# Batch 1's fourth turn, the first two pairs' sums and batch 3's turns moved by a few slots in a fused attention and MoE kernel

## The chip, the cores and the metric

The kernel runs on one core of a Trainium2 chip. The metric is the device time of one execution in microseconds (us). All times of single instructions below come from one profiled execution. The engines are called PE (matrix products; PEld is its weight load), DVE (VectorE), ACT (ScalarE), POOL (GpSimd) and SP (SyncE, which issues DMAs here).

## What is computed

Attention over 8 batches, 8 heads, 576 positions of 64 numbers, with a sliding window of 128 positions and a linear bias per head, then two matrix products with an ELU between them.

```python
def _attn_ref(q, k, v) -> np.ndarray:
    B, H, S, D = q.shape
    window = 128
    scale = 1.0 / np.sqrt(D)
    scores = scale * np.matmul(q, k.transpose(0, 1, 3, 2))
...
    mask = (rel >= 0) & (rel < window)
    scores = np.where(mask, scores + bias[None], -1000000000.0)
    scores = scores - np.max(scores, axis=-1, keepdims=True)
    attn = np.exp(scores)
    attn = attn / (np.sum(attn, axis=-1, keepdims=True) + 1e-09)
    return np.matmul(attn, v).astype(np.float32)

def _moe_ref(x, w_in, w_out) -> np.ndarray:
    h = x @ w_in
    alpha = 1.0
    g = np.where(h > 0.0, h, alpha * (np.exp(np.minimum(h, 0.0)) - 1.0))
    return (g @ w_out).astype(np.float32)
```

The attention output, 4608 tokens of 512 numbers, is x; w_in is 512 by 2048 and w_out is 2048 by 512.

## The kernel before

Attention and the two products are interleaved by hand. The order is a list of slots, numbered from 0. A slot holds, in this order: exponentials of scores (`before`), one hidden step (`HID`, function `hidden`), the ELU of the slot before (`done`, which calls `elu`), the slot's tasks (`at`, in the order in which they were entered; `at_once` puts a task in front of all those entered so far), output products (`OUT`) and what comes last (`after`). Every engine takes its instructions in the order in which the slots issue them, and a semaphore holds an instruction until its inputs are there and its target is free.

The parts of a slot that matter here:

- **Hidden step** (L305): 512 columns of x times w_in, into one of two PSUM banks, hp0 and hp1, in turn. ACT turns it into e, by two activations (L312, L313) in the slots of the set `SOFT`, or by one (L315) with POOL's clamp (L316) in the others. DVE's `elu` (L323) makes g from e and the bank, and so frees the bank for the step two slots later.
- **Output products** of a pair of token tiles (L393, `product`). Pair n is 256 tokens; seven products take the place of eight, from sums of blocks of g (`sums`: S1 to S4 on DVE, L354) and of w_out (`quarters`: T1 to T4). The order of a pair's products is 1, 2, 6, 5, 7, 3, 4, seven block products to a slot. Product 6 needs S2, product 5 S1, product 7 S3, product 3 S4. ACT copies some results to U tiles (L396), and `combine` adds them into the output tile (C11, C12, C22; L354 with the target ob), which SP sends out (L412).
- **Attention.** The scores of a unit of 128 keys go to banks spa, sp2, sp3 (L176 for batch 1, L225 later); ACT takes exponentials (L205 and L210, L233 and L236); DVE multiplies them by a table (`first_weigh`, L216; `weigh`, L241); PE multiplies them with the values (L253, L271) with the sum of the weights as a last column; DVE makes the norm (rden, L259 or L276) and scales (xn, L260 or L277).
- **turn** (L281 to L290) transposes the finished tile xn into xT, the hidden steps' input: through PE (L289) and a copy by ACT (L290), or by a DMA transpose from SP (L285). Batch 1's tiles 0 to 3 go through PE, tile 3 by the bank sp3.
- **turn_qk** (L145): DVE transposes q and k of batches 2 and up in 32 by 32 blocks; four instructions for a batch: k in two halves, q in two halves.

Pair n has its slots from 15 + 8n on: pair 2 has slots 31 to 39. Pair 1 has the nine slots (19, 20, 21, 22, 23, 25, 27, 29, 30). A pair's S1 stands in the slot before its first, S2, S3 and S4 in its slots number 1, 3 and 4 (counted from 0), C22 in number 8. Batch 1's units are worked on in slots 18 to 32; batch 2's units start in slot 31 and batch 3's in slot 48. `START` gives the slot in which the scores of a batch's first unit are issued, `TURN` the slots in which q and k of batches 2 and 3 are turned; later batches take slots from `START`. POOL issues the loads of q, k and v.

Of the kernel before, what the change touches and what calls it, by code (L numbers as in the profile page):

```python
# [18 lines left out]
def kernel(  # L19
# [9 lines left out]
    nc = tc.nc  # L29
# [47 lines left out]
    sp = [spa[:, 0, :], spa[:, 1, :]] + [ps_s.tile([128, 512], F32, name=f"sp{i}", tag=f"sp{i}") for i in (2, 3)]  # L77
    hp = [ps_h.tile([128, 512], F32, name=f"hp{i}", tag=f"hp{i}") for i in range(2)]
    av = ps_v.tile([128, 512], F32, name="av", tag="av")
# [69 lines left out]
    with tc.manual_schedule():  # L149
# [343 lines left out]
        def at(s, f, *a):  # L493
            tasks.setdefault(s, []).append((f, a))

        def at_once(s, f, *a):
            tasks.setdefault(s, []).insert(0, (f, a))

        def after(s, f, *a):
            late.setdefault(s, []).append((f, a))  # L500
# [81 lines left out]
        for u, a0, a1, d in ((0, 18, 19, 2), (1, 20, 21, 2), (2, 22, 24, 0), (3, 26, 28, 0)):  # L582
            for half, a in enumerate((a0, a1)):
                at(a, first_scores, 1, u, half, d * half)
                at(a, first_expo, 1, u, half, d * half, 0, 256)
                at(a + 1, first_weigh, 1, u, half)
                at(a + 2, values, 1, u, half, av if half else sp[2])
            at(a1 + 3, turn, 1, u, nc.scalar.copy, (av, av, av, sp[3])[u])
        at(25, turn_first, 1, 1, 1, 0, av, nc.scalar.copy)
        at(30, values, 1, 4, 0, sp[2])  # L590
        at(31, values, 1, 4, 1)
# [2 lines left out]

        START = [None, None, 31, 48, 66, 83, 100, 117]

        TURN = [None, None, (22, 24, 25, 28), (40, 42, 44, 46)]
        REST = 32, 33, 36, 37
        for b in range(2, B):
            for u in range(4):  # L600
# [13 lines left out]
            for n in range(4):  # L614
                piece = (b, int(n < 2), n % 2)
                if b == 2:
                    m = 4 if n < 2 else 6
                    at(TURN[b][n], turn_qk, *piece, 0, m)
                    at(REST[n], turn_qk, *piece, m, R)
                else:  # L620
                    at(TURN[b][n] if b == 3 else a + 4 * n, turn_qk, *piece)
            for n in range(8):
# [8 lines left out]
        for n in SEVEN:  # L631
            s = 15 + 8 * n
            ps = (19, 20, 21, 22, 23, 25, 27, 29, 30) if n == 1 else range(s, s + 9)
            if n < 2 * NTB - 1:
                for d, i in ((-1, 1), (1, 2), (3, 3), (4, 4)):
                    at_once(ps[d] if d > 0 else ps[0] - 1, sums, n, i)
                after(ps[2], combine, n, "C11")
                after(ps[6], combine, n, "C12")
                at_once(ps[8], combine, n, "C22")
                for d in range(8):  # L640
                    OUT[ps[d]] = [(product, (n, i, j, j + 1)) for i, j in turns[7 * d:7 * d + 7]]
            else:
                at_once(s - 3, sums, n, 3)
                for i in (2, 1):
                    at_once(s - 2, sums, n, i, 0, 6)
                    at_once(s - 1, sums, n, i, 6, 8)
                at(s - 1, product, n, 1)
                OUT[s] = [(product, (n, 2)), (combine, (n, "C11")), (sums, (n, 4)), (product, (n, 6)), (product, (n, 5))]
                OUT[s + 1] = [(product, (n, 7)), (product, (n, 3)), (combine, (n, "C22")), (combine, (n, "C12")),
                              (product, (n, 4)), (last_out, (n,))]  # L650
# [48 lines left out]
```

## Time and profile before

| | us |
|---|---|
| median of 4 runs | 311.41 |
| lowest, highest | 310.97, 313.57 |
| the profiled execution | 311.59 |
| its span (first to last instruction) | 309.8 |

TensorE's granted clock is 1.00 in all of it. Two of the costliest groups of instructions, and the ones that the change moves:

```profile
L305 PE MATMUL hp<-xT,wi 128*128 128x256 f16 (+3 forms) x1488 | 144.3, 245 | 1.3 <-DVE g L323 1.0
L323 DVE SCALAR_TENSOR_TENSOR g<-e,hp 128x512 f16<-128x512 f32 x138 | 93.8, 679 | 23.3 <-ACT e L313 12.8
L354 DVE TENSOR_TENSOR S<-g 128x1024 f16<-128x1024 f16 (+2 forms) x35 | 23.6, 673 | 0.8 <-PE op L393 0.2
```

A line of a group gives the source line, the engine, the operation, target and inputs with their sizes, the count, then the busy time in us and the mean of one in ns, and last the idle time of the engine just before, with what ended most of it. A line of a timeline gives start, duration, engine, source line and tiles, and in square brackets how long the engine had been idle and which instruction released it. A line of the chain of waits gives the start and length of a piece of the chain that ended last. In a table of stretches each engine has its busy time and its number of instructions, followed by the clock, the share of the DMA engines and the rate in GB/s.

Durations of neighbours on one engine overlap a little, so the distance from one start to the next is what an instruction takes from its engine: the g of 0.68 us takes 0.60. In time, slot 18 begins at about 48 us, slot 31 at 69, slot 35 at 79, slot 48 at 105.

### The profile page before, as it was taken

What the parts mean: (1) busy time and instruction counts of PE and PEld (TensorE: products, weight loads), DVE (VectorE), ACT (ScalarE), POOL (GpSimd) and SP (SyncE); (2) the same over time, 40 slices, a digit from 0 to 9 for tenths busy, and PEclk for the clock granted to TensorE, in tenths of its full rate; (3) what the DMA queues carried; (4) which work ended last, traced back from release to release, by engine and by line L of the source; (5) the groups of instructions that cost most, each with busy time, mean ns of one, the idle gap of its engine ahead of it and who ended that gap; (6) DMA issues with size and microseconds to landing.
All of it is one profiled execution on the core that took longest, in us unless ns stands there. A gap on an engine that the chain in (4) does not pass through costs nothing.

```text
span 309.8 us, 9820 instructions
## 1 busy us (share of the span) xinstructions
PE 299.7 (97%) x4071; PEld 256.2 (83%) x4071; DVE 257.9 (83%) x498; ACT 241.8 (78%) x446; POOL 108.7 (35%) x163
## 2 busy tenths in 40 slices
PE   7899999998999999999999999999999999999995
PEld 5688875797888888988888888888899888898884
DVE  4646879988989999897989998989998788886782
ACT  4576678677888698879797889788888797968871
POOL 8847858374251415140706060706000001010000
PEclk9999999999999999999999999999999999999999
DMA  9999999999094949495979997999630302230103
GB/s 97 177 200 199 202 187 185 104 115 114 19 153 72 134 73 148 55 142 69 112 89 122 126 96 84 129 130 111 66 98 5 95 17 87 19 97 0 70 27 111
DMA packets 96509, 32.04 MB, mean 103 GB/s; under 512 B 83920, under 2 KB 91984, under 8 KB 96464
## 3 DMA queue, kind: packets, MB, share of 16 engines
q0 software_dynamic: 75920, 18.36, 64.1%
q1 hardware_dynamic: 20400, 12.98, 17.5%
q8 instruction: 32, 0.52, 0.7%
q14 instruction: 13, 0.11, 0.1%
q10 hardware_dynamic: 144, 0.07, 0.1%
HBM read 36.70 MB, written 9.44 MB: 149 GB/s over the span
## 4 chain that ended last, share of the span: by engine, by line
PE 76%; DVE 7%; ACT 7%; DMA 3%; issue 3%; POOL 3%; POOLq 0%; ACTq 0%; DVEq 0%
PE hp L305 34%; PE op L393 13%; PE av L393 13%; PE spa L225 4%; DVE g L323 3%; DMA s<-in_q_dram 3%; PE spa L271 3%; PE sp L393 2%; ACT EX L236 2%; PE op L329 1%; POOL e L316 1%; PE sp L305 1%; ACT e L315 1%; PE sp L253 1%; ACT e L312 1%
## 5 line engine op out<-in xcount | busy, mean ns | idle before, releaser
L305 PE MATMUL hp<-xT,wi 128*128 128x256 f16 (+3 forms) x1488 | 144.3, 245 | 1.3 <-DVE g L323 1.0
L305 PEld LDWEIGHTS <-wi 128*128 128x128 f16 x1600 | 119.7, 98 | 18.3 <-issue 6.7
L323 DVE SCALAR_TENSOR_TENSOR g<-e,hp 128x512 f16<-128x512 f32 x138 | 93.8, 679 | 23.3 <-ACT e L313 12.8
L316 POOL TENSOR_SCALAR e<-e 128x512 f32<-128x512 f32 x44 | 28.1, 639 | 157.8 <-ACT e L315 152.9
L312 ACT ACTIVATE e<-hp 128x512 f32<-128x512 f32 x98 | 58.6, 598 | 28.7 <-PE hp L305 24.2
L313 ACT ACTIVATE e<-e 128x512 f32<-128x512 f32 x100 | 63.1, 631 | 3.2
L393 PEld LDWEIGHTS <-S 128*128 128x128 f16 x544 | 51.4, 98 | 6.1 <-issue 0.5
L393 PEld LDWEIGHTS <-g 128*128 128x128 f16 x408 | 38.2, 98 | 4.8 <-issue 0.6
L241 DVE TENSOR_TENSOR EX<-EX,TAB 128x1024 f16<-128x1024 f16 x48 | 33.0, 687 | 6.4 <-ACT EX L236 3.7
L114 POOL DMA_DIRECT2D VP<-in_v_dram x40 | 34.5, 874 | 2.1 <-DMA s<-in_k_dram 1.0
L315 ACT ACTIVATE e<-hp 128x512 f32<-128x512 f32 x40 | 24.1, 601 | 10.4 <-PE hp L305 10.4
L393 PE MATMUL op<-T,S 128*128 128x256 f16 x200 | 30.0, 273 | 0.0
L233 ACT ACTIVATE EX<-spa 128x1024 f16<-128x1024 f32 x24 | 24.6, 1025 | 4.4 <-PE spa L225 4.1
L393 PE MATMUL av<-T,S 128*128 128x256 f16 x176 | 26.4, 272 | 0.1
L236 ACT ACTIVATE EX<-sp 128x512 f16<-128x512 f32 x48 | 26.0, 596 | 0.0
L354 DVE TENSOR_TENSOR S<-g 128x1024 f16<-128x1024 f16 (+2 forms) x35 | 23.6, 673 | 0.8 <-PE op L393 0.2
L393 PE MATMUL op<-wo,g 128*128 128x256 f16 x128 | 19.2, 273 | 0.1
L393 PE MATMUL av<-wo,g 128*128 128x256 f16 x120 | 18.0, 273 | 0.0
L277 DVE TENSOR_TENSOR xn<-spa,rden 128x512 f16<-128x512 f32 x24 | 16.6, 692 | 0.8
L108 POOL DMA_DIRECT2D st<-in_k_dram x24 | 16.2, 686 | 2.8 <-DMA s<-in_q_dram 2.1
L108 POOL DMA_DIRECT2D st<-in_q_dram x24 | 15.9, 666 | 0.8 <-DMA VP<-in_v_dram 0.6
L271 PE MATMUL spa<-VP,EX 128*128 128x65 f16 x336 | 15.2, 193 | 0.1
(139 smaller groups left out, 379.7 us busy)
## 6 DMA issues: line engine op xcount, KB each, us to landing
out_dram<-ob SPq DMA_DIRECT2D x35, 256.0 KB, 2.5
VP<-in_v_dram POOLq DMA_DIRECT2D x32, 128.0 KB, 5.6
st<-in_k_dram POOLq DMA_DIRECT2D x24, 144.0 KB, 5.1
st<-in_q_dram POOLq DMA_DIRECT2D x24, 144.0 KB, 5.9
wi<-in_moe_w_in_dram POOLq DMA_DIRECT2D x4, 512.0 KB, 12.0
wo<-in_moe_w_out_dram POOLq DMA_DIRECT2D x4, 512.0 KB, 11.2
VP<-in_v_dram POOLq DMA_DIRECT2D x8, 64.0 KB, 5.8
s<-in_k_dram POOLq DMA_DIRECT2D x1, 512.0 KB, 13.2
```

Of the source, the lines that this page charges most:

```text
L108: nc.gpsimd.dma_start(st[b][32 * g:32 * g + 32, w, :, :, :, :].rearrange("p h n j d -> p (h n) (j d)"), (q, k)[w][b, 2 * g:2 * g + 2, :, : ...
L114: nc.gpsimd.dma_start(VP[b % 2][0:p, n, :, 0:D], v[b, :, 128 * n:128 * n + p, :].rearrange("h p d -> p h d"))
L233: nc.scalar.activation(unit(b, u)[:, 0:2, :, :], spa.rearrange("p g (h c) -> p g h c", h=2), AF.Exp, scale=0.125)
L236: nc.scalar.activation(unit(b, u)[:, g, :, :], sp[g].rearrange("p (h c) -> p h c", h=2), AF.Exp, scale=0.125)
L241: V.tensor_tensor(out=e, in0=e, in1=TAB[:, int(u == 3), 2 * gp:2 * gp + 2, :, :], op=ALU.mult)
L305: nc.tensor.matmul(p[:, l * w + u0:l * w + u1], w_in_sb[:, c, fc * 128:(fc + 1) * 128], xT[:, c, x0:x0 + u1 - u0], start=(c == 0), stop=(c ...
L312: nc.scalar.activation(e[:, 0:n], p[:, 0:n], AF.Relu, scale=-1.0)
L313: nc.scalar.activation(e[:, 0:n], e[:, 0:n], AF.Exp, scale=-1.0)
L315: nc.scalar.activation(e[:, 0:n], p[:, 0:n], AF.Exp)
L316: nc.gpsimd.tensor_scalar(out=e[:, 0:n], in0=e[:, 0:n], scalar1=1.0, scalar2=0.0, op0=ALU.min, op1=ALU.max)
L323: V.scalar_tensor_tensor(out=gs[t][:, f0:f0 + nf, c0:c0 + w], in0=sh(es.pop((t, c0, f0))), scalar=1.0, in1=sh(hps.pop((t, c0, f0))), op0=A ...
L393: nc.tensor.matmul(o, a[:, j, :], b[:, j, :], start=j == 0 and i in (1, 2, 5), stop=j == 7, skip_group_check=True)
```

## The change

Three edits, each in the order alone:

```diff
-            at(a1 + 3, turn, 1, u, nc.scalar.copy, (av, av, av, sp[3])[u])
+            at(a1 + 3 + u // 3, turn, 1, u, nc.scalar.copy, (av, av, av, sp[3])[u])
...
-        TURN = [None, None, (22, 24, 25, 28), (40, 42, 44, 46)]
+        TURN = [None, None, (22, 24, 25, 28), (35, 39, 43, 47)]
...
-                    at_once(ps[d] if d > 0 else ps[0] - 1, sums, n, i)
+                    (at_once if n > 2 else at)(ps[d] if d > 0 else ps[0] - 1, sums, n, i)
...
-                at_once(ps[8], combine, n, "C22")
+                (at_once if n > 2 else at)(ps[8], combine, n, "C22")
```

- Batch 1's tile 3 (u is 3, so u // 3 is 1) is turned in slot 32 instead of 31: four transposes on PE and one copy on ACT. The hidden steps that read this tile begin in slot 34.
- Batch 3's k halves are turned on DVE in slots 35 and 39 instead of 40 and 42, its q halves in 43 and 47 instead of 44 and 46.
- The sums S1 to S4 and C22 of pairs 1 and 2, the second and third pair, come behind the other tasks of their slot instead of ahead of them: behind the weights and norms of the attention units. From pair 3 on they stay ahead.

One consequence for what is computed: the turn in slot 32 writes the first half of bank sp3 after batch 2's first unit has put its scores there (end of slot 31) and before the exponential of slot 33 reads them. For one head of that unit the exponentials are then taken of the transposed bits, not of the scores. The number and size of all instructions stay as they were.

## The prediction

> **What bounds the kernel now.** I read the page first, then the stretches by time, then the chain of waits and the timelines of DVE, ACT and PE where the change acts. Page, busy time and the chain by engine:
>
> ```profile
> PE 299.7 (97%) x4071; PEld 256.2 (83%) x4071; DVE 257.9 (83%) x498; ACT 241.8 (78%) x446; POOL 108.7 (35%) x163
> ...
> PE 76%; DVE 7%; ACT 7%; DMA 3%; issue 3%; POOL 3%; POOLq 0%; ACTq 0%; DVEq 0%
> ```
>
> PE carries the end, so the change can only be worth the gaps of PE in the slots it touches. The stretches (PE, PEld, DVE, ACT, POOL busy) show where these are:
>
> ```profile
> 48.00:58.00 10.00, 9.28 (x114) 6.45 (x111) 9.38 (x21) 7.44 (x13) 6.04 (x8) 1.00 1.93 178
> 58.00:69.00 11.00, 11.00 (x226) 10.14 (x224) 9.08 (x19) 8.63 (x15) 7.82 (x12) 1.00 0.80 95
> 69.00:83.00 14.00, 12.84 (x197) 10.90 (x194) 12.57 (x26) 11.08 (x21) 3.58 (x5) 1.00 0.68 78
> 83.00:94.00 11.00, 11.00 (x144) 9.67 (x142) 9.76 (x20) 9.40 (x18) 6.34 (x9) 1.00 1.22 133
> 94.00:107.00 13.00, 12.51 (x171) 10.71 (x172) 12.61 (x26) 9.54 (x19) 4.70 (x7) 1.00 0.74 91
> ```
>
> The slots touched by the pairs (18 to 24 and 30 to 39) and by batch 3's turns (35 to 47) lie in rows one, three and five. PE is idle there for 0.72, 1.16 and 0.49 us, 2.4 in all: a ceiling of 0.8% of the span. In the same rows DVE is 94%, 90% and 97% busy, so DVE, not PE, is the engine with no room. The largest gap, from the whole timeline:
>
> ```profile
> 68.50 0.69 DVE L323 SCALAR_TENSOR_TENSOR g<-e,hp 128x512 f16<-128x512 f32 x1 [0.51 <-POOL e L316]
> ...
> 69.22 0.69 DVE L354 TENSOR_TENSOR S<-g 128x1024 f16<-128x1024 f16 x1
> ...
> 69.33 1.06 POOL L316 TENSOR_SCALAR e<-e 128x512 f32<-128x512 f32 x1 [0.24 <-ACT e L315]
> 69.83 0.83 DVE L354 TENSOR_TENSOR ob<-U,U 128x256 f32<-128x256 f32 x1
> ...
> 70.59 0.17 DVE L259 RECIPROCAL rden<-av 128x4 f32<-128x4 f32 x1
> ...
> 70.79 0.42 DVE L260 TENSOR_TENSOR xn<-av,rden 128x256 f16<-128x256 f32 x1
> ...
> 71.27 0.34 PE L289 MATMUL sp<-ident,xn 128*128 128x128 f16 x3 [0.92 <-DVE xn L260]
> ```
>
> Pair 2's first sum S1 and pair 1's C22 stand ahead of batch 1's norms, and PE's turn of the fourth tile waits 0.92 for them. In slots 42 to 46, by the chain of waits:
>
> ```profile
> 95.14 0.40 DVE xn L277
> 95.54 0.21 issue
> 95.75 0.77 DVE KT L145
> 96.52 0.58 DVE g L323
> 97.10 0.04 issue
> 97.15 1.03 PE hp L305 x8
> ...
> 102.99 0.69 DVE xn L277
> 103.68 0.21 DVE QT L145
> 103.89 0.39 issue
> 104.28 0.66 DVE g L323
> 104.95 0.04 issue
> 104.99 1.03 PE hp L305 x8
> ```
>
> Here a turn of batch 3 on DVE (0.77) delays the elu g that frees the bank of PE's next hidden step: twice a third of a microsecond.
>
> **The change part by part.** No instruction is added or removed. The instruction order of the changed program shows 493 instructions on DVE and 442 on ACT as before; POOL's and SP's orders are the same, so no DMA is passed. I replay the order with steps from one start to the next in the timeline: g, S and weigh 0.60, rden 0.20, xn of 256 columns 0.34, ob 0.34, full turn 0.69; on PE a hidden step 0.89, a product 0.11; on ACT L290 0.46.
>
> *A, pair 1 (slots 18 to 24).* S2 (50.19) goes behind the norms and the second weigh of unit 0. That norm waits for PE until 50.96 anyway, so the weigh still starts at 51.52. S2 then ends near 52.8; its product starts at 53.04. The next norms and weigh slip 0.11 (PE +0.1). S3 at 54.08 no longer stands ahead of unit 1's second weigh, which would end 0.25 earlier, so the gap before PE's values at 55.98 (0.47) halves. But S3 now ends near 56.6, and its product, at 56.66 before, waits for that. Taken: 0. Bounds: -0.35 (if S3 fits in) to +0.15 (the slip stays). S4 and C22 are used one or more slots later; their cover is that distance.
>
> *B, slots 30 to 35.* DVE after the g of 68.50: rden, xn, rden, xn at 69.22, 69.42, 69.76, 69.96; C22 at 70.30, S1 at 70.64, the g of slot 30 at 71.25, ending 71.93 (72.3 before). PE no longer turns in slot 31: values at 70.13 instead of 71.45, products 70.37, scores 71.23, hidden step of slot 32 not at its natural 71.79 but at 72.0, when that g is done; 73.11 before. So 1.1 earlier. What is late next: the turn's four matmuls (0.22) now come after that step, and ACT's copy L290 has left a place where ACT idled (0.98 before the 73.22 exponential) for one where ACT runs without a gap until 79.9: behind it are U1, the exponentials L236 of sp2 and sp3, then two pairs L312/L313. L236 starts at 75.0 to 75.1 instead of 75.63, the weigh at 76.15 (76.75), C11 at 77.2 (77.79), and PE's product that waits for C11 at 77.6 (78.22). Of 1.1 us, 0.5 goes to L290's step, and 0.6 remains.
>
> One size is open, C22's. The row has 0.83, every other such ob 0.41 or 0.42, while POOL's e beside it took 1.06 instead of 0.61. The Trainium skill ("SBUF — State Buffer", section "SBUF: two separate sides") says that a VectorE operation with two SBUF inputs and a GpSimd one that reads SBUF hold a shared port pair in turn, for the whole instruction. By that e, now beside norms that read PSUM, ends near 70.0, before C22 starts at 70.30, and C22 costs 0.41: -0.6. By the row alone, 0.83 again: -0.2. I take -0.6; bounds -0.9 (the whole wait of L289) to +0.45 (rival 2). The same rule speaks against the change further on: with PE and DVE shifted unequally, the e of slots 36, 44 and 45 would start during a weigh; in before they ran beside others and took 0.61. The rule would hold each until the weigh ends, 0.3 to 0.45; the rows of such meetings (e at 64.14 and 67.67, during a weigh) show 0.84 and 0.80, so 0.2 each. I take the rows' 0.2.
>
> *C, batch 3's turns.* Slot 35 takes a turn of 0.69 ahead of S4 and g. With B's lead the g of slot 34 ends near 80.2, K's turn 80.8, S4 81.4, g 82.1; PE wants that bank at 82.2. The 0.39 and 0.28 that DVE idles at 82.39 and 83.65 pay for it. S4's product comes 0.55 into slot 36, at 81.9: covered. Slot 39's turn lies behind slot 38's g, which PE needs only 0.9 later. In slot 42 nothing stands between xn and g any more: PE's step of slot 44 starts at its natural 96.73 less 0.6, not 97.15: another 0.4. In slot 46 likewise 0.33. Together a lead of 1.3 at slot 48. It can't all stay: DVE has as much to do up to slot 48 as before, and Q's last turn is now in slot 47, right ahead of that slot's g. DVE's own lead is what its idle times give. The g of slot 45 (101.42) came after two waits for e and can be 1.0 early, less 0.2 for the port: 0.8. From there to the g of slot 48 (108.16) DVE runs without a break, and PE needed that g 0.12 after its end: a lead of 0.9. So C adds 0.3. Bounds: -0.7 to +0.2 (all idle time of DVE used, or Q's turn holding batch 3's first scores). K's and Q's loads cover: issued by 70.34, and landing takes 8.1 at most.
>
> *Later.* From slot 49 on both programs are alike, and PE is 92.75 of 93 and 99.8 of 100 us busy: a lead is kept. The fourth tile's turn writes half of bank sp3 between batch 2's scores and their exponential; an exponential's time does not depend on its numbers in any row, so nothing is charged.
>
> Sum: 0 - 0.6 - 0.3 = -0.9 us. Against the profiled execution, 311.59 (span 309.8 and 1.8 around it): 310.7. That run lies 0.18 over the median of 311.41, so 310.5.
>
> **The rivals.**
> 1. *DVE is the bound, and the lead is eaten.* For it: 12.61 of 13 us busy in the fifth row. B's lead falls to 0.2 (C22 at 0.83), C gives it back: 311.2, between 310.9 and 311.5. Against it: 2.4 us of waits that the timeline shows on DVE between 70 and 102, which an earlier PE shortens.
> 2. *L290 in front of the exponentials: slower.* Place: ACT in slot 32. Price: 0.46, since U1, L236, the weigh, C11 and PE's product follow it one by one. It decides if the hidden step of slot 32 starts less than 0.46 earlier, thus if g of slot 30 ends after 72.6 (a longer C22, or a later e). With nothing of the lead left it costs up to 0.45, and with A's +0.15: 312.0. Against it: 0.7 us between 71.93 and that point.
> 3. *The change does not do what it says*: pair 1 gains nothing because its norms wait for PE, not DVE. That is in the sum already; without B's gain too it is 311.4, counted with rival 1.
>
> **How the numbers follow.** Forecast 0.62 (own range 309.9 to 311.0), rivals 1 and 3 together 0.24, rival 2 0.14. Predicted 310.5. The range, 309.6 to 312.0, reaches down nearly to the three lower bounds together (-1.95, 309.5) and takes in rival 1 whole and rival 2 up to its price; what it leaves out is part C at its upper bound on top of rival 2. About 1% (3.1 us) is what a measurement of this kernel can tell from no change. Faster by that needs more than the 2.4 us of gaps: 0.02. Slower by it needs a wait that comes back in each of many slots, where the diff touches three short stretches: 0.04. Within 1%: 0.94.
>
> **What would show it.** B right: no wait of L289 for xn, C22 at 0.41, the hidden step of slot 32 about 1.1 earlier, PE's product after C11 0.6 earlier. C right: no wait of L305 for g at slots 44 and 48, and about 0.9 of lead at 109. A right: S3 the last wait in slot 23. Wrong if PE gains at 56 or if L236 of slot 33 is not earlier. The forecast as a whole is wrong if PE shows new gaps after 110, which I hold for alike.

## The result, and the profile after

| | before | after |
|---|---|---|
| median, us | 311.87 (64 runs) | 310.98 (43 runs) |
| lowest, highest | 310.92, 313.57 | 309.88, 313.55 |
| profiled execution, its span | 311.59, 309.8 | 313.29, 311.5 |

The ratio of after to before is 0.9971, 95% interval 0.996 to 0.9981: 0.9 us less. With more runs than the prediction had, the median of before is 311.87, not 311.41, so the forecast 310.5 stands 0.5 below what was measured although the difference of 0.9 is the one forecast.

The profiled execution of the changed kernel is longer than that of before, and this has to be understood first. Its first hidden steps already start 2.7 us late, in code that the change does not touch. So all comparisons below are made slot by slot: the start of the hidden step's first matmul, counted from the hidden step of slot 17 in the same execution (44.49 us before, 47.16 after), minus the same for before. From slot 1 to slot 17 this difference is within 0.02 us in all kernels of this study; what happens ahead of slot 1 drops out. Kernels with the same edits in a stretch agree there to 0.02 as well (slots 32 to 36 of the change and of two of the kernels below).

| slot | 24 | 32 | 33 | 35 | 36 | 43 | 44 | 46 | 48 | 50 | 76 | 149 |
|---|---|---|---|---|---|---|---|---|---|---|---|---|
| after, us | +0.03 | -1.22 | -1.01 | -0.75 | -0.62 | -0.61 | -1.02 | -0.79 | -1.11 | -0.93 | -0.95 | -0.97 |

The stretches of before that had PE's gaps, in the changed kernel (the same slots, shifted by the start and by what was gained; columns as before):

```profile
50.70:60.70 10.00, 9.50 (x114) 6.36 (x110) 8.99 (x21) 7.44 (x13) 4.35 (x6) 1.00 1.73 159
71.70:85.00 13.30, 13.06 (x197) 10.80 (x193) 12.42 (x27) 11.09 (x21) 3.13 (x5) 1.00 0.76 83
96.10:108.70 12.60, 12.55 (x174) 10.59 (x172) 11.74 (x25) 9.49 (x19) 5.01 (x7) 1.00 0.78 94
```

PE idles 0.50, 0.24 and 0.05 us there (0.72, 1.16 and 0.49 before). This idle time is not the gain: in the first row 0.22 of it is gone although slot 24 starts no earlier, because the wait is now one of the weight loads (shown under part A), which PE's column does not count. Slot 31 in the timeline of after, PE, DVE and ACT:

```profile
71.20 0.69 DVE L323 SCALAR_TENSOR_TENSOR g<-e,hp 128x512 f16<-128x512 f32 x1 [0.50 <-POOL e L316]
...
71.81 0.18 DVE L259 RECIPROCAL rden<-av 128x4 f32<-128x4 f32 x1
...
72.83 0.41 PE L253 MATMUL av<-VP,EX 128*128 128x65 f16 x8
72.90 0.41 DVE L354 TENSOR_TENSOR ob<-U,U 128x256 f32<-128x256 f32 x1
...
73.83 0.67 DVE L323 SCALAR_TENSOR_TENSOR g<-e,hp 128x512 f16<-128x512 f32 x1
...
74.56 1.05 PE L305 MATMUL hp<-xT,wi 128*128 128x128 f16 x16
```

The norm follows g at once, no wait stands beside PE's values, C22 (ob) takes 0.41 instead of 0.83, and the hidden step of slot 32 starts 2.62 us after that of slot 31 (71.94) instead of 3.87. It starts 0.06 after the end of the g of slot 30: that is its last wait. In slot 44:

```profile
97.20 0.69 DVE L277 TENSOR_TENSOR xn<-spa,rden 128x512 f16<-128x512 f32 x1
97.80 0.68 DVE L323 SCALAR_TENSOR_TENSOR g<-e,hp 128x512 f16<-128x512 f32 x1
...
98.80 1.05 PE L305 MATMUL hp<-xT,wi 128*128 128x256 f16 x8
```

No turn stands between xn and g, and g is done 0.3 before PE asks.

### The profile page after: what moved, and what is told of

It reads as the page before. It is cut to its first block, busy times and chain, and to the rows that moved or that the text cites. A ratio compares the mean times of both kernels' runs of the same rounds, so it can differ in the third digit from the quotient of the medians.

```text
span 311.5 us, 9820 instructions
## 1 busy us (share of the span) xinstructions
PE 302.8 (97%) x4071; PEld 258.3 (83%) x4071; DVE 258.0 (83%) x498; ACT 241.8 (78%) x446; POOL 108.4 (35%) x163
## 4 chain that ended last, share of the span: by engine, by line
PE 73%; DMA 7%; DVE 6%; ACT 5%; POOL 4%; issue 3%; POOLq 0%; DVEq 0%; ACTq 0%
PE hp L305 33%; PE op L393 12%; PE av L393 12%; DMA VP<-in_v_dram 4%; PE spa L225 4%; PE spa L271 3%; DVE g L323 2%; DMA s<-in_q_dram 2%; PE sp L393 2%; ACT EX L236 2%; POOL e L316 1%; DMA xT<-xn 1%; ACT e L315 1%; PE sp L253 1%; POOL st L108 1%
```

## The experiments

The first question was which edit gives the 0.97, and whether they need each other; the second, what takes back the part of the lead that slots 33 to 36, 46 and 50 lose; the third, whether a version is to be had without these losses. Every table row below is counted as above. Ratios to before have their 95% intervals; intervals of 0.3% or so are wider than most of these parts, so the slot count carries the verdicts, and it is from one profiled execution of each kernel. In all kernels but the first below, the interval of the ratio contains what the slots say at slot 149.

**Pair 1's sums alone.**

```diff
-                    at_once(ps[d] if d > 0 else ps[0] - 1, sums, n, i)
+                    (at if n == 1 else at_once)(ps[d] if d > 0 else ps[0] - 1, sums, n, i)
```

> Pair 1's S1 to S4 behind weights and norms, nothing else. Theory (part A is worth 0): PE's values of slot 23 start 0.2 to 0.25 us earlier than before, then product 7 waits for the later S3, and the hidden step of slot 24 starts within 0.05 us of before, counted from the hidden step of slot 17. Whole time 0 (-0.1 to +0.1). Rival (the whole gap of 0.47 in slot 23 goes): -0.3 to -0.45 us from slot 24 on.

Measured: +0.03 at slots 24 to 48, +0.10 at slot 149; ratio 1.0022 (1.0006 to 1.0037). The slots say 0.03%, the times 0.2%; the part of the program ahead of slot 17, which is the same code, took 45.17 us in its profile and 44.49 in that of before, a difference as large as what the times show. That the other executions started late too is not shown. By the slots part A is worth nothing, as expected.

**The turn alone** (slot 32 instead of 31).

```diff
-            at(a1 + 3, turn, 1, u, nc.scalar.copy, (av, av, av, sp[3])[u])
+            at(a1 + 3 + u // 3, turn, 1, u, nc.scalar.copy, (av, av, av, sp[3])[u])
```

> Only batch 1's fourth tile turned in slot 32 instead of 31 (as in the change, its transposes overwrite half of a score bank). Theory: nothing is gained, since PE's values of slot 31 wait for the same norm on bank av, and ACT's copy L290 (step 0.46) now stands ahead of the exponentials L236: the hidden step of slot 36 starts 0.2 to 0.3 us later than before, whole time +0.2 (0 to +0.45). Rival (the move of the turn is what frees PE): -0.6 us.

Measured: slot 32 -0.18, slot 33 +0.04, slot 36 +0.31, slot 149 +0.37; ratio 1.0003 (0.9987 to 1.0019). Its timeline, PE and ACT:

```profile
71.04 0.40 PE L253 MATMUL av<-VP,EX 128*128 128x65 f16 x8 [0.97 <-DVE xn L260]
...
74.97 0.57 ACT L290 COPY xT<-sp 128x512 f16<-128x512 f16 x1
```

PE waits as long as before, now as the values of the fifth tile for the same norm, through bank av. From slot 32 to slot 35 the kernel goes from -0.18 to +0.31: the copy's place costs 0.49, rival 2's mechanism, seen alone.

**Pair 2's sums and both C22 alone**, the turn still in slot 31.

```diff
-                    at_once(ps[d] if d > 0 else ps[0] - 1, sums, n, i)
+                    (at if n == 2 else at_once)(ps[d] if d > 0 else ps[0] - 1, sums, n, i)
...
-                at_once(ps[8], combine, n, "C22")
+                (at_once if n > 2 else at)(ps[8], combine, n, "C22")
```

> Pair 2's S1 to S4 and the C22 of pairs 1 and 2 behind norms; the fourth tile is still turned in slot 31, batch 3's q and k in the old slots. Theory: PE's wait of 0.92 for xn goes, but batch 2's scores in bank sp3 wait for ACT's copy L290 of the turn, so the hidden step of slot 32 is about 0.55 earlier instead of 1.25, and with L290 out of ACT's row in slot 32 all of it is kept: slot 36 -0.55 (-0.4 to -0.65), whole time the same. Rival (the wait is only moved to sp3 in full): -0.1 to 0.

Measured: slot 32 -0.46, slot 36 -0.33, slot 149 -0.26; ratio 0.9985 (0.9963 to 1.0007). PE's wait in its timeline:

```profile
71.34 0.27 PE L225 MATMUL sp<-QT,KT 32*128 32x256 f16 x1 [0.37 <-ACT xT L290]
```

The wait for the norm is gone, and a new one takes its place: batch 2's scores for bank sp3, which L290 still reads. The expectation (-0.55) missed by 0.22 at slot 36: 0.09 of it is there at slot 32, the rest comes in slot 35 (-0.45 to -0.32) and is S3 (below).

**Batch 3's turns alone**, and **all but these**.

```diff
-        TURN = [None, None, (22, 24, 25, 28), (40, 42, 44, 46)]
+        TURN = [None, None, (22, 24, 25, 28), (35, 39, 43, 47)]
```

> Only batch 3's q and k turned in slots 35, 39, 43, 47. Theory (DVE's idle time of 0.39 and 0.28 in slots 36 and 37 pays for the first turn, and the parts are not additive): slots 37 to 43 within 0.1 us of before, slot 44 -0.4, slot 48 -0.7, then the g of slot 48 takes some back: whole time -0.45 (-0.3 to -0.55), more than the -0.3 that this part adds on top of the others. Rival (without the lead of slot 32 the first turn makes slots 37 and 38 late, and this part alone gains nothing): -0.1 to +0.3.

> The change without its edit of batch 3's turns (parts A and B; as in the change, the fourth tile's transposes overwrite half of a score bank). Alone, the sums gave 0.33 and the move of the turn lost 0.31 at slot 36. Theory (the two need each other: with sums out of the way the turn's copy holds bank sp3, with the turn moved the sums still hold bank av): slots 32 to 36 as in the whole change (-1.2, then -0.62), and this lead stays: -0.6 (-0.55 to -0.65) from slot 50 on. Rival (the parts add): 0.

Measured, turns alone: slot 38 +0.05, slot 44 -0.36, slot 48 -0.57, slot 50 -0.27, slot 149 -0.30; ratio 0.9994 (0.9976 to 1.0012). The first turn in slot 35 is paid for without the others' lead, as the theory had it, but the part is worth 0.3 either way, not the 0.45 that was expected of it alone. Measured, all but these: slot 36 -0.61, slot 50 -0.60, slot 149 -0.55; ratio 0.9987 (0.9973 to 1.0). So pair 2's sums (-0.33) and the turn's move (+0.31) give -0.61 together at slot 36 and near 0 as a sum of the two; A with B (-0.60) and C (-0.27) do add, to -0.87 at slot 50, where the whole has -0.93.

**The turn in another bank**, spa, which batch 2's exponential has left by then; no score is overwritten.

```diff
-            at(a1 + 3 + u // 3, turn, 1, u, nc.scalar.copy, (av, av, av, sp[3])[u])
+            at(a1 + 3 + u // 3, turn, 1, u, nc.scalar.copy, (av, av, av, sp[0])[u])
```

> The whole change with the fourth tile's transposes in bank spa instead of sp3, so that no score is overwritten. PE then waits for the exponential L233 to leave spa, 0.15 to 0.2 us in slot 32. Theory (in slots 32 to 35 ACT's row and what hangs on it sets PE's time): slot 33 -0.8 to -0.85 instead of -1.0, but slot 36 within 0.1 of the whole change (-0.5 to -0.62), end -0.85 to -0.97. Rival (PE itself is the limit there): all later slots 0.15 to 0.2 worse, end -0.75 to -0.8.

Measured: slot 33 -0.78, slot 36 -0.62, slot 149 -0.87; ratio 0.9974 (0.9961 to 0.9988). PE lost 0.23 in slot 32 and had it back at slot 35 (-0.74, the change -0.75): ACT's row, not PE, sets the time there. The overwritten scores are not what the gain comes from.

**The turn by DMA**, in slot 30, on the whole change.

```diff
-            at(a1 + 3 + u // 3, turn, 1, u, nc.scalar.copy, (av, av, av, sp[3])[u])
+            at(a1 + 3 - u // 3, turn, 1, u, *((nc.scalar.copy, av) if u < 3 else ()))
```

> The whole change, but the fourth tile is turned by a DMA transpose from SP in slot 30, as the fifth is: no transposes on PE, no copy L290 on ACT, no score overwritten. Theory (L290 in ACT's row of slot 32 costs 0.46): if the DMA lands before slot 34 needs the tile (about 5.2 us after the norm, by the median of these DMAs, just in time), slot 33 is at -1.2, slot 36 at -0.95 to -1.1, and the end at -1.1 to -1.3, since DVE has no more idle time than that. If it lands 1 to 2 us later, PE waits for it in slot 34 and the end is at -0.3 or worse. Rival (ACT's row is not the limit): slot 36 stays at -0.6 to -0.8.

Measured: slot 33 -1.24, slot 36 -1.11, slot 48 -1.72, slot 50 -1.41, slot 149 -1.44; ratio 0.9958 (0.9941 to 0.9974). Against the change, 0.49 more at slot 36: the price of L290 and the four transposes in slot 32 (the step of L290 is 0.46). The end is 0.14 better than the best that was expected. The DMA was early enough: issued at 70.35, it landed 5.1 later, 0.4 before slot 34 began (75.88). The 5.2 that the expectation calls the median of these DMAs is not in the profile of before; its median from issue to landing is 4.0, the range 2.3 to 7.5.

**Batch 3's turns where DVE waits**, on the whole change.

```diff
-        TURN = [None, None, (22, 24, 25, 28), (35, 39, 43, 47)]
+        TURN = [None, None, (22, 24, 25, 28), (33, 36, 41, 44)]
...
-                    at(TURN[b][n] if b == 3 else a + 4 * n, turn_qk, *piece)
+                    (at_once if b == 3 else at)(TURN[b][n] if b == 3 else a + 4 * n, turn_qk, *piece)
```

> The whole change, but batch 3's turns stand in slots 33, 36, 41 and 44 ahead of the slot's other tasks, where the trace of the change shows DVE waiting (0.73, about 0.4, 0.56 and 0.4 us) for ACT's exponentials or POOL's clamp (as in the change, half of a score bank is overwritten). Theory (part C takes from DVE's idle time, and the 0.2 lost at slots 46 and 50 are DVE running behind): slot 36 -0.62 as in the change, slot 48 about -1.1, and slot 50 keeps it: end -1.1 to -1.25. Rival (the loss at slot 50 is not from DVE's turns): -0.95 as in the change.

Measured: slot 36 -0.62, slot 46 -0.89, slot 48 -1.23, slot 50 -1.22, slot 149 -1.21; ratio 0.9957 (0.9943 to 0.9971). What slot 50 took back is gone: the last of q's turns stood in slot 47, right ahead of that slot's g. (Batch 4's first turn stays in slot 48 here, and costs nothing. K's turns are moved too; the last kernel below has them back, and loses nothing at slot 50 either.) Part of the loss at slot 46 stays. The timeline of the change, DVE, POOL and PE:

```profile
100.27 0.68 DVE L241 TENSOR_TENSOR EX<-EX,TAB 128x1024 f16<-128x1024 f16 x1
...
100.66 0.76 POOL L316 TENSOR_SCALAR e<-e 128x512 f32<-128x512 f32 x1 [8.63 <-ACT e L315]
101.45 0.69 DVE L323 SCALAR_TENSOR_TENSOR g<-e,hp 128x512 f16<-128x512 f32 x1 [0.51 <-POOL e L316]
...
102.29 0.77 PEld L305 LDWEIGHTS <-wi 128*128 128x128 f16 x8 [0.33 <-DMA xT<-xn]
102.30 1.05 PE L305 MATMUL hp<-xT,wi 128*128 128x256 f16 x8
```

The same place in this kernel:

```profile
97.24 0.76 POOL L316 TENSOR_SCALAR e<-e 128x512 f32<-128x512 f32 x1 [8.63 <-ACT e L315]
98.03 0.69 DVE L323 SCALAR_TENSOR_TENSOR g<-e,hp 128x512 f16<-128x512 f32 x1 [0.51 <-POOL e L316]
...
98.78 1.03 PE L305 MATMUL hp<-xT,wi 128*128 128x256 f16 x8
```

POOL's e begins during a weigh and takes 0.76, not 0.61 as in before, where it met no weigh. Here the hidden step of slot 46 starts 0.06 after the end of g and loses 0.10; that is e's part. In the change it starts 0.16 after the end of g (102.14), since a second wait ends later: the DMA that turns the tile of slot 42, issued at 97.92, lands at 102.25. That is the other 0.1 of the 0.21.

**Both of these**, and then **S3 as well**: pair 2's S3 in front again, the turn of batch 2's first k piece from slot 22 to 23.

```diff
-                    (at_once if n > 2 else at)(ps[d] if d > 0 else ps[0] - 1, sums, n, i)
+                    (at_once if n > 2 or (n, i) == (2, 3) else at)(ps[d] if d > 0 else ps[0] - 1, sums, n, i)
...
-        TURN = [None, None, (22, 24, 25, 28), (33, 36, 41, 44)]
+        TURN = [None, None, (23, 24, 25, 28), (33, 36, 41, 44)]
```

> Both: the fourth tile turned by DMA in slot 30, and batch 3's turns ahead of the tasks of slots 33, 36, 41 and 44. The DMA alone on the change ended at -1.44 us, of which slots 46 and 50 had taken back 0.1 and 0.22; the holes alone at -1.21, with 0.12 taken back at slot 46. Theory (the two losses are DVE running behind and do not depend on slot 32): slot 36 -1.11, slot 48 -1.7, end -1.65 to -1.75. Rival (a larger lead meets the same limit of DVE): -1.45 as with the DMA alone.

> As the one before, with two edits for S3, which in both pairs is the last wait of product 7: pair 2's S3 goes back in front of slot 34's other tasks, and the turn of batch 2's first k piece (0.36) moves from slot 22, ahead of pair 1's S3, to slot 23. Theory (part A's gain of 0.22 in slot 23 and 0.13 in slot 35 are lost to S3 alone): slot 24 at -0.18 to -0.22, slot 36 0.3 earlier than without them, end -1.9 to -2.05. Rival (ACT's copy U6, done at about the same time as S3, holds product 7): slot 24 at 0 to -0.05, end -1.7 to -1.85.

Measured, both: slot 33 -1.22, slot 35 -0.89, slot 36 -0.77, slot 149 -1.30; ratio 0.9948 (0.9928 to 0.9968). Theory and rival both missed: this is less than the DMA alone by the slots. DVE in its slot 33:

```profile
74.93 0.68 DVE L323 SCALAR_TENSOR_TENSOR g<-e,hp 128x512 f16<-128x512 f32 x1
75.53 0.77 DVE L145 STREAM_TRANSPOSE KT<-st 128x576 int32<-128x576 int32 x1
76.22 0.65 DVE L241 TENSOR_TENSOR EX<-EX,TAB 128x1024 f16<-128x1024 f16 x1
```

No wait is left around k's turn. The wait of 0.73 that the turn was to fill was L290's doing, and with L290 gone the turn is on the path. Measured with the S3 edits: slot 24 -0.22, slot 36 -1.16, slot 149 -1.65; ratio 0.9944 (0.9928 to 0.9959). S3 gives back what was expected of it (0.22 and 0.13: the lead no longer falls from slot 35 to 36), but k's turn in slot 33 keeps the end behind both figures that had been named.

**S3 by itself**: part A alone with the k piece moved.

```diff
-        TURN = [None, None, (22, 24, 25, 28), (40, 42, 44, 46)]
+        TURN = [None, None, (23, 24, 25, 28), (40, 42, 44, 46)]
```

> Part A alone (pair 1's sums behind weights and norms) with the turn of batch 2's first k piece moved from slot 22 to slot 23, so that S3 ends 0.36 us earlier; the rest as before. Theory (S3 alone eats part A's gain): slot 24 at -0.18 to -0.22 us and the same at the end. Rival (U6 or the values are the limit): 0, as in the run of part A alone (+0.03).

Measured: slot 24 -0.22, slot 48 -0.17, slot 149 -0.11; ratio 0.9991 (0.9977 to 1.0005). Its timeline, DVE and PE:

```profile
54.41 0.68 DVE L216 TENSOR_TENSOR EX<-EX,TAB 128x1024 f16<-128x1024 f16 x1
55.01 0.68 DVE L354 TENSOR_TENSOR S<-g 128x1024 f16<-128x1024 f16 x1
...
55.15 0.41 PE L253 MATMUL av<-VP,EX 128*128 128x65 f16 x8
...
55.84 0.49 PE L393 MATMUL op<-T,S 128*128 128x256 f16 x3
```

S3 is done at 55.69, product 7 starts 0.69 after the values, without a wait; in the change the same distance is 0.93 (58.43 to 59.36).

**The version with the largest lead** by the slots: the DMA, the S3 edits, q's turns ahead of the tasks of slots 41 and 44, k's behind those of slots 35 and 39.

```diff
-        TURN = [None, None, (23, 24, 25, 28), (33, 36, 41, 44)]
+        TURN = [None, None, (23, 24, 25, 28), (35, 39, 41, 44)]
...
-                    (at_once if b == 3 else at)(TURN[b][n] if b == 3 else a + 4 * n, turn_qk, *piece)
+                    (at_once if b == 3 and n > 1 else at)(TURN[b][n] if b == 3 else a + 4 * n, turn_qk, *piece)
```

> The version with all edits, but k of batch 3 is turned where the change has it, behind the tasks of slots 35 and 39; only q's turns stand ahead of the tasks of slots 41 and 44. Theory (the wait of DVE in slot 33 was made by ACT's copy L290; with the DMA in L290's place there is no room there, and k's turn in it cost 0.35 in slot 35): slot 36 about -1.5, slot 48 about -2.2, end -2.0 to -2.15, ratio about 0.993. Rival (k's turn is paid for somewhere in any case): -1.65, as before.

Measured: slot 24 -0.22, slot 36 -1.49, slot 44 -1.84, slot 46 -1.72, slot 48 -2.05, slot 149 -2.01; median 309.48 against 311.68, ratio 0.9942 (0.9923 to 0.9961). Its stretches for the same slots:

```profile
47.40:57.20 9.80, 9.38 (x114) 6.42 (x111) 8.79 (x20) 7.44 (x13) 5.83 (x8) 1.00 1.95 181
68.50:81.00 12.50, 12.47 (x191) 10.60 (x191) 12.12 (x25) 10.35 (x20) 3.10 (x5) 1.00 0.90 96
91.70:104.40 12.70, 12.70 (x174) 10.86 (x175) 11.84 (x24) 9.71 (x19) 5.02 (x7) 1.00 0.81 100
```

In the second and third PE has no gap left to speak of. With k's turns back behind the tasks of slots 35 and 39 the 0.33 is there again (slot 36 -1.49, -1.16 with the turn in slot 33). No score is overwritten in this version.

## Why the prediction was right

- **Part A, 0.** Right, and by the step that was named. DVE and PE of slots 22 and 23, before and then in the change:

```profile
54.08 0.69 DVE L354 TENSOR_TENSOR S<-g 128x1024 f16<-128x1024 f16 x1
...
55.98 0.41 PE L253 MATMUL av<-VP,EX 128*128 128x65 f16 x8 [0.47 <-ACT U L396]
...
56.66 0.49 PE L393 MATMUL op<-T,S 128*128 128x256 f16 x3
```

```profile
57.69 0.68 DVE L216 TENSOR_TENSOR EX<-EX,TAB 128x1024 f16<-128x1024 f16 x1
58.29 0.44 DVE L145 STREAM_TRANSPOSE KT<-st 128x256 int32<-128x256 int32 x1
...
58.43 0.41 PE L253 MATMUL av<-VP,EX 128*128 128x65 f16 x8
58.65 0.65 DVE L354 TENSOR_TENSOR S<-g 128x1024 f16<-128x1024 f16 x1
...
59.35 0.22 PEld L393 LDWEIGHTS <-S 128*128 128x128 f16 x3 [0.35 <-DVE S L354]
59.36 0.50 PE L393 MATMUL op<-T,S 128*128 128x256 f16 x3
```

With the 2.67 of the start taken off, PE's values start 0.22 earlier (55.76), and product 7, at 56.69, no earlier than before: its weight load waits for the end of S3. That S3 alone does it is shown by the run with the k piece moved: -0.22.

- **Part B, -0.6.** The sum is right (-0.62 at slot 36), the way to it nearly. The hidden step of slot 32 came 1.22 earlier (1.1 said). C22's open size went the way of the lock rule, 0.41, and the last section shows the rule at work. After that the lead shrank to 0.75 at slot 35 (0.6 said for PE's product after C11): 0.47 went to L290's step (0.5 said). Then 0.13 more went in slot 35, for which the sum had nothing: pair 2's S3 now stands behind the norm, and product 7 waits for it. PE's weight loads in the change say so:

```profile
82.19 0.22 PEld L393 LDWEIGHTS <-S 128*128 128x128 f16 x3 [0.24 <-DVE S L354]
```

The prediction looked for S3 in pair 1 and not in pair 2. The two misses, 0.15 too little lead and 0.13 of loss left out, cancel: that B's sum fits to 0.02 is luck, its mechanism is not. That the whole of B needs both edits was in its steps, and the two runs with one edit each show it.

- **Part C, -0.3.** -0.31 was measured, from -0.62 at slot 36 to -0.93 at slot 50. The gains are those that were named: 0.41 at slot 44 (0.4 said) and 0.33 at slot 48 (0.33 said). So is the limit, DVE's own lead. With the 2.67 taken off, the g of slot 45 starts 0.84 earlier than before (103.25 against 101.42; 0.8 said) and the g of slot 48 0.85 (109.98 against 108.16), and that is what PE waits for at slot 50:

```profile
109.98 0.64 DVE L323 SCALAR_TENSOR_TENSOR g<-e,hp 128x512 f16<-128x512 f32 x1
...
110.67 1.03 PE L305 MATMUL hp<-xT,wi 128*128 128x256 f16 x8
```

The step starts 0.05 after the end of this g, and the lead falls from 1.11 to 0.93 (from 1.3 to 0.9 said). The last kernel, with k's turns as in the change and q's elsewhere, keeps its lead there (-2.05 at slot 48, -2.04 at slot 50): it was q's turns. Not in the sum is the loss of 0.21 at slot 46, e and the late DMA, where e had been charged to DVE's lead only. It does not change the end: the kernel with the turn in bank spa, with the same order on DVE, loses 0.11 there, has -1.21 at slot 48 and comes to -0.91 at slot 50. POOL's e took 0.76 and 0.77 in slots 44 and 45, where 0.61 and the rows' 0.2 had been said; in slot 36, where the same had been said, it took 0.61.

- **Later, nothing.** Right: from slot 50 to 149 the difference moves by 0.04.

- **Rival 1** (DVE eats the lead) is seen in its small form, the 0.18 of slot 50. **Rival 2** is real: 0.49 from slot 32 to 35 in the turn-only kernel, and 0.49 of L290 and the transposes against the DMA (0.46 said). It did not decide because the sums' move brought 1.22 first: the g of slot 30 ended at 71.83 of before's time, not after 72.6. **Rival 3** is right that pair 1 gains nothing, but not for the reason it gives: with S3 out of the way 0.22 is gained, so the wait of its norms for PE is not what stops it.

What stays open: why the differences of the single edits drift by up to 0.1 between slots 50 and 149, and how often the DMA of slot 42 lands as late as in the profile of the change; in the seven other kernels with the same meeting of e and weigh, slot 46 loses 0.10 to 0.11. One profiled execution of each does not tell.

## What to carry to other kernels

An instruction that delays a consumer can be one of two or three that hold it in turn, through different buffers: moving the sums alone uncovered the copy's hold on sp3, moving the turn alone left the norm's hold on av, and only both together gave the gain. Before an instruction is put into an idle place of an engine, ask what makes that place idle; if another edit takes the cause away, the place goes with it. For changes below half a per cent, compare two profiles from a common point behind the loads, step by step, and use the times to confirm the sum.

## What the runs showed of the hardware

The times of before scatter from 310.9 to 313.6 us. In the 14 profiled executions of this study the hidden step of slot 17 starts between 43.7 and 47.2 us, and from slot 1 to slot 17 all take the same time within 0.02. The time of each is 311.59, plus its difference from before at slot 17, plus its slot count at 149, to within 0.16 us: what scatters in these 14 lies ahead of slot 1. The latest start is the profile of the change. Its PE waits for a part of q to land:

```profile
8.61 0.64 PE L136 MATMUL hp<-ident,s 64*64 64x64 f16 x16 [1.54 <-DMA s<-in_q_dram]
```

and the granted clock is at half from 8.5 us to past 14.5 (the number behind the five engines in a stretch; first before, then after):

```profile
8.50:10.50 2.00, 1.98 (x43) 1.46 (x42) 1.33 (x5) 1.36 (x2) 2.00 (x3) 1.00 1.06 164
...
10.50:12.50 2.00, 1.58 (x25) 1.01 (x22) 1.44 (x5) 1.62 (x4) 1.79 (x7) 1.00 1.48 198
```

```profile
8.50:10.50 2.00, 1.89 (x40) 1.70 (x40) 0.79 (x3) 0.58 (x1) 1.02 (x3) 0.50 1.28 178
10.50:12.50 2.00, 2.00 (x26) 1.54 (x24) 1.62 (x4) 1.27 (x2) 1.88 (x4) 0.50 1.37 173
```

The same sixteen transposes take 0.64 us there and 0.44 in before. None of the other 13 profiles shows a clock below 1.00 between 5 and 16.5 us, although PE waited 1.29 to 1.32 us for the same part of q in three of them (slot 17 then starts at 44.80, 44.81 and 45.04). In the run of pair 1 alone q came nearly as late as here, its transposes starting at 8.34 against 8.61, at full clock, and slot 17 starts at 45.17. Put beside that, by estimate the late load accounts for 0.95 of the 2.67 us (45.17 - 44.49, and 0.27 for the rest), and the other 1.7 lie in the stretch at half clock. The Trainium skill ("TensorE: Matmul & The Clock Gate", section "Part 1: The HAM clock gate (the "warmup" mystery)") has the clock fall to half after an idle window of some 3.4 us; the longest wait seen here is 1.54 us. What set the clock down is open. It is not the only such execution: the profile of the change has a mean clock of 0.989, and of the executions whose clock is on record 8 of 120 of before have 0.995 or less and are its eight longest (313.07 to 314.22 us, the others up to 312.58), as are 7 of 44 of the change (312.11 to 313.55, the others up to 311.95). Where their clock was down was not traced.

The lock between POOL and DVE that the prediction weighed can be read from the rows. Alone, e takes 0.61. When it begins during a weigh or an S of 1024 columns, it ends 0.47 to 0.48 after the end of that instruction, in all 111 meetings of the 14 profiles that overlap by more than 0.14; up to 0.14 it takes its 0.60 to 0.62. So e is held for the whole of the other's instruction, less some 0.13: 0.76 in slot 44 of the change (overlap 0.29), 0.84 for the deepest meeting with a weigh (0.37). The same explains C22 in before: S ends at 69.91, e at 70.39, 0.48 later, and C22 at 70.66, 0.27 after e.
